# Half of the fifth-chunk adds as accumulating transfers, value sums in four batches, and the second tile's copies on swapped engines

## The chip, the core and the metric

The kernel runs on one core of a Trainium2 chip. The core has five engines that run in parallel, each through its own queue in order: TensorE (PE, with its weight load PEld), VectorE (DVE), ScalarE (ACT), GpSimd (POOL) and SyncE (SP), which only issues transfers. They meet at semaphores. The metric is the device time of one execution in microseconds (us); all times below are in us unless marked ns. The kernel before takes 266.07, the median of three runs (266.06 to 266.19).

## The reference

A layer norm feeds a sliding attention and a gated product; both are added to the input.

```python
xn = _layernorm(x)                       # x: [1, 2048, 640], bf16
qkv = xn @ wqkv                          # 32 heads of 20
idx = pos[:, None] - 2 * arange(8)       # each position sees 8 earlier ones, 2 apart
logits = einsum("bhsd,bhswd->bhsw", q, kg) * 20 ** -0.5     # masked where idx < 0
o = einsum("bhsw,bhswd->bhsd", softmax(logits), vg)
a = o.reshape(1, 2048, 640) @ wo
b = ((xn @ w_gate) * (xn @ w_up)) @ w_down                  # inner width 1536
return x + a + b
```

## The kernel before

**An order written by a planner.** The program is built by a small list scheduler (`Sched`, lines 50 to 351). Every operation is given to it with a planned cost (`occ`, `acc`), and what it reads and writes. Threads (Python generators) offer tasks with a priority; `run` (line 235) picks, engine by engine, the task that can start first by the planned costs, and among those within a small patience the one of best priority. What comes out is a fixed list of instructions for each engine, with a semaphore wait wherever a result of another engine is needed. The planned costs thus set the order alone; on the chip an instruction waits for its data and for nothing else. `slack` on a task moves its planned readiness later, `keep` asks that so many PSUM banks stay free besides its own. `lock=True` keeps DVE passes over 16-bit data in SBUF and POOL's adds from running at the same time.

**Tiles.** The 2048 positions are 16 tiles of 128 (`TS`) and four blocks of 512 (`JB`, index j); the 640 features are five chunks of 128 (`NCH`, index c). PSUM has eight banks of 512 fp32 columns.

**Start.** A tile t is loaded, DVE takes its statistics, ACT the square root, and DVE applies the norm (`front`, line 566). For tiles 0 to 3 TensorE transposes the five chunks and they are copied from PSUM to `XNT`. For tiles 0 and 1 this goes in two parts, chunks 0 and 1, then 2 to 4 (`PARTS`, line 502), and `COPY` (line 503) names the engine of each part. The first projections (`proj_group`, `spread`, line 730) follow a tile's parts. Ahead of all this `warm` (line 680) lets TensorE multiply zeros.

**Logits.** A query is multiplied with its eight shifted keys on DVE, in two halves r of four shifts. For blocks 0 and 1 a product of one chunk is one pass in bf16 (`narrow`, L880), and five chunks are added by TensorE (L1012), through a matrix that also sums over a head. For blocks 2 and 3 (`QUAD`, line 424) only chunk 4 is done so. Chunks 0 to 3 are multiplied straight from PSUM into fp32 (`wide`, L929), in quarters (r, q0) of two shifts each, and are added by POOL, until one tile for each r is left for TensorE:

- the sum of chunks 0 and 1 (`sum32`, p = 0): an add on POOL (L955), or an accumulating transfer SBUF to SBUF issued from POOL's queue (L951), as `BY_DMA` says;
- then the fifth chunk's product `z` (bf16) is added to it (L966); `LAST_DMA`, which is empty, names the quarters where a transfer does it (L962);
- the sum of chunks 2 and 3, or of the running sum with chunk 2 (`close`, with `sum32` at p = 1), again by POOL or by a transfer;
- the closing add (L988), which writes bf16.

The logits of blocks 2 and 3 are one task for TensorE (`JOIN`, line 1468; `logits`, line 995), with a slack of 2.0. Softmax runs over two blocks at a time (`softmax`, line 1042).

**Values.** A unit u is a block and a chunk, u = 5j + c. DVE multiplies the shifted values with the attention weights (L1191), POOL adds pairs of shifts (two adds per unit, L1196), and TensorE sums over the shifts left (L1250), whose result ACT evicts into `OT` (L1259). `BATCH` (line 1105) says after which units TensorE takes a batch of sums (`sums`, line 1237). A batch takes one PSUM bank per unit at once, and two more banks hold attention weights until the last unit is multiplied.

**Gate, up and down.** `gu` (line 1287) takes the gate and up projections of block j in twelve slices m (L1314), ACT evicts the gate, DVE multiplies (L1323, from PSUM). For slices in `FAST` (line 1467) ACT evicts the up part as well, and DVE multiplies in bf16 from SBUF (L1361). `dn` (line 1387) takes the down projection in pieces of a tile and 320 columns: twelve matmuls over `WD`, then five over `WO` with `OT` (L1416). A down piece keeps the banks of the next batch of sums free as long as the block's `OT` is not complete. Blocks 0 to 2 are added onto a copy of x in the output by an accumulating transfer from POOL's queue (`add_out`, line 1439); block 3 adds x on DVE (L1429) and is stored.

Of the kernel before, what the change touches and what calls it, by code (L numbers as in the profile page):

```python
# [15 lines left out]
NF = 12  # L16
# [5 lines left out]
TS = 128  # L22
JB = 512
HB = 1024
QB = 256
# [24 lines left out]
class Sched:  # L50
# [78 lines left out]
    def op(self, eng, fn, r=(), w=(), dma=False, name="", occ=None, lat=None, lock=False, nbytes=0, mode=0, group=None, extra=0.0, acc=0.0, land=None):  # L129
# [19 lines left out]
        if dma:  # L149
            self.t[eng] = start + (0.48 if occ is None else occ)  # L150
            if acc:
                self.t_acc = max(self.t_acc, start + 3.8) + acc
                X.end = self.t_acc
            else:
                self.t_data = max(self.t_data, start + 1.2) + nbytes / 280e3
                X.end = self.t_data + 0.8 + extra
# [199 lines left out]
def build_kernel(nc, A_x, A_wqkv, A_wo, B_x, B_w_gate, B_w_up, B_w_down, out):  # L356
# [68 lines left out]
    LAST_DMA = ()  # L425
# [77 lines left out]
    COPY = (("act", "act"), ("act", "dve"))  # L503
# [176 lines left out]
    def warm(n):  # L680
        for _ in range(n):
            op("pe", lambda e: e.matmul(PS[:, 7, 0:QB], ZERO[:, 0:128], ZERO[:, 0:QB], start=True, stop=True),
               r=[ZERO[:]], w=[PS[:, 7, :]], name="warm", occ=0.2 if n > 3 else 0.12)
# [80 lines left out]
    def proj_qk():  # L764
# [8 lines left out]
        for t in (4, 6):  # L773
            yield have("xnt", t + 1)
            for items in ([(0, 0, 2)], [(1, 0, 2)], [(0, 2, 2)], [(1, 2, 2)], [(0, 4, 1), (1, 4, 1)]):
                K.spawn(proj_group(items, t * TS, 2 * TS, 11 + t * 0.1, None))
# [68 lines left out]
    def products():  # L845
        rows = {j: [] for j in range(NJ)}
        joined = []
        holds = {}
        for at, (j, kind) in enumerate(ORDER):
# [4 lines left out]
            else:  # L854
                if len(QUAD.get(j, ())) == 2 and j not in holds and (j, "w") == ORDER[at + 1]:
                    yield from fetch(j, 0, holds.setdefault(j, {c: [] for c in range(4)}))
                for r in (1, 0):
                    for c in range(NCH - 1 if r in QUAD.get(j, ()) else 0, NCH):
                        yield from narrow(j, r, c, rows[j])
            if len(rows[j]) == 10 - 4 * len(QUAD.get(j, ())) and kind == ("w" if j in QUAD else "n"):  # L860
                if j in JOIN:
                    joined.append((j, rows[j]))
                    if len(joined) == len(JOIN):
                        K.spawn(logits(*joined))
                else:
                    K.spawn(logits((j, rows[j])))
# [43 lines left out]
    def wide(j, slots, hold):  # L910
        halves = [(r, q0) for r in QUAD[j] for q0 in (0, 2)]
        acc, parts = {}, {1: [], 0: []}
        lastc = {r: [n, 0] for n, _, r in slots}
        slots.clear()
# [32 lines left out]
    def sum32(j, r, q0, p, a, b, last=None):  # L947
        x, y = PRD32[a][:], PRD32[b][:]
        name = f"qsum{j}_{r}_{q0}_{p}"
        if (r, q0) in BY_DMA[p]:  # L950
            yield Task("pool", lambda: op("pool", lambda e: e.dma_start(x, y, accum_op=ALU.add), r=[x, y], w=[x], dma=True,  # L951
                                          name=name, occ=0.88, acc=3.4), r=[x, y], w=[x], prio=4)
# [8 lines left out]
        if (r, q0) in LAST_DMA:  # L961
            yield Task("pool", lambda: op("pool", lambda e: e.dma_start(x, z, accum_op=ALU.add), r=[x, z], w=[x], dma=True,  # L962
                                          name=name + "c", occ=0.88, acc=3.4), r=[x, z], w=[x], prio=4)
# [141 lines left out]
    BATCH = (4, 9, 14, 17, 19)  # L1105
# [131 lines left out]
    def sums(us):  # L1237
# [26 lines left out]
        yield Task("pe", go, r=[SV[sv_of[u]][:] for u in us], prio=9.7, banks=len(us), slack=0.7)  # L1264
# [135 lines left out]
    def dn_piece(j, t, nb, rows, c0, c1):  # L1400
# [38 lines left out]
        def add_out():  # L1439
# [3 lines left out]
                             name=f"oadd{j}", occ=0.88, acc=4))  # L1443
# [23 lines left out]
    FAST = [(1, m) for m in range(6, NF)] + [(2, m) for m in range(4, 8)]  # L1467
    JOIN = (2, 3)
# [26 lines left out]
    warm(18)  # L1495
# [64 lines left out]
```

## Time and profile before

| | |
|---|---|
| median of three runs | 266.07 |
| the profiled execution's own time | 266.25 |
| its span | 264.4 |
| PE busy | 259.8 (98% of the span), 1748 matmuls |
| DVE busy | 220.1 (83%) |
| POOL busy | 160.8 (61%) |
| ACT busy | 111.9 (42%) |
| value products L1191 on DVE | 54, 90.8 |
| value adds L1196 on POOL | 40, 94.4 |
| fifth-chunk adds L966 on POOL | 8, 19.5 |
| accumulating transfers L951 | 8 of 512 KB, median 5.1 to landing |

A busy share is an average over the whole span. The chain of work that ended last is followed back from the last instruction: at each step to what released it, or to the instruction before it on its engine. In the rows of the order in time the columns are start, busy time, engine, line, operation, output and inputs with their shapes (partitions x elements), a count of merged instructions, and in brackets the idle time of the engine just before and what ended it. A group's row gives the count, then busy time in total, the mean ns of one, and the idle time before them. Matmuls are pipelined, and the end of a matmul in the records is modelled; the pace is read from start to start.

### The profile page before, as it was taken

How to read it: one execution, taken by the hardware profiler on the slowest of the kernel's cores; microseconds unless marked ns; L12 is line 12 of the kernel's file. 1: busy time of each engine (PE TensorE's matmuls, PEld its weight loads, DVE VectorE, ACT ScalarE, POOL GpSimd, SP SyncE). 2: the span in 40 equal slices, each digit the busy share in tenths (PEclk: the TensorE clock that was granted, in tenths of full speed). 3: DMA queues.
4: the chain of work that ended last, by engine and by line, in shares of the span. 5: the costliest groups of instructions: out<-in, count | busy, mean ns of one | idle time of the engine just before them, and what ended most of it. 6: DMA issues, size and time to landing. Idle time of an engine off the chain costs nothing.

```text
span 264.4 us, 4405 instructions
## 1 busy us (share of the span) xinstructions
PE 259.8 (98%) x1748; PEld 151.8 (57%) x1748; DVE 220.1 (83%) x259; ACT 111.9 (42%) x203; POOL 160.8 (61%) x97
## 2 busy tenths in 40 slices
PE   7999999999999999999999999999999999999996
PEld 4896975444444444444444444477646775776675
DVE  4787899999998799778779999999899998995032
ACT  3468987556612221224268652531235134213100
POOL 3000000000599998899973575599999999999300
DMA  6964679960379995470249425736586537600711
GB/s 207 373 211 84 126 95 383 443 233 18 121 136 187 234 222 111 85 144 1 61 132 308 90 47 121 152 86 157 153 166 138 147 93 124 129 1 0 102 50 50
DMA packets 39685, 37.83 MB, mean 143 GB/s; under 512 B 15697, under 2 KB 37329, under 8 KB 39633
## 3 DMA queue, kind: packets, MB, share of 16 engines
q1 hardware_dynamic: 36688, 31.32, 44.3%
q0 software_dynamic: 2736, 6.16, 13.5%
q8 instruction: 13, 0.21, 0.4%
q10 hardware_dynamic: 240, 0.07, 0.1%
q14 instruction: 8, 0.06, 0.1%
HBM read 25.07 MB, written 7.23 MB: 122 GB/s over the span
## 4 chain that ended last, share of the span: by engine, by line
PE 96%; DMA 2%; DVE 1%; SPq 0%; ACT 0%; issue 0%
PE PS L1314 39%; PE PS L1416 28%; PE PS L698 23%; PE PS L1012 2%; PE PS L1250 2%; PE PS L730 2%; DMA XST<-in_A_x_dram 2%; DVE STATS L574 0%; PE PS L642 0%; SPq L480 0%; ACT XNT L655 0%; DVE XNS L603 0%; ACT SD L584 0%; DVE FB L1429 0%; DVE MV L577 0%
## 5 line engine op out<-in xcount | busy, mean ns | idle before, releaser
L1196 POOL TENSOR_TENSOR SV<-PV 128x1024 bf16<-128x1024 f32 x40 | 94.4, 2384 | 17.1 <-DVE PV L1191 5.9
L1191 DVE TENSOR_TENSOR PV<-VX,PS 128x1024 f32<-128x1024 bf16 (+1 forms) x54 | 90.8, 1730 | 1.5 <-POOL SV L1196 1.5
L698 PE MATMUL PS<-XNT,WQKV 128*128 128x512 bf16 (+2 forms) x390 | 60.8, 316 | 0.0
L1314 PE MATMUL PS<-XNT,WG 128*128 128x512 bf16 x240 | 59.7, 379 | 0.0
L1314 PE MATMUL PS<-XNT,WU 128*128 128x512 bf16 x240 | 59.6, 379 | 0.0
L698 PEld LDWEIGHTS PS<-XNT,WQKV 128*128 128x128 bf16 x390 | 37.9, 112 | 21.9 <-ACT LOG L1023 0.8
L1314 PEld LDWEIGHTS PS<-XNT,WG 128*128 128x128 bf16 x240 | 23.2, 98 | 28.9 <-DVE XNT L1323 0.8
L1314 PEld LDWEIGHTS PS<-XNT,WU 128*128 128x128 bf16 x240 | 23.5, 98 | 28.0
L929 DVE TENSOR_TENSOR PRF<-PS,KT 128x1024 f32<-128x1024 f32 x32 | 37.9, 1218 | 0.3 <-PE PS L698 0.3
L955 POOL TENSOR_TENSOR PRF<-PRF,PRF 128x1024 f32<-128x1024 f32 x8 | 22.0, 2755 | 20.6 <-DVE LOG L1072 20.6
L703 ACT ACTIVATE HT<-PS 128x512 bf16<-128x512 f32 x24 | 14.3, 597 | 34.5 <-PE PS L1314 34.5
L1416 PE MATMUL PS<-WD,HT 128*128 128x320 bf16 x192 | 28.7, 299 | 0.0
L703 ACT ACTIVATE FB<-PS 128x320 bf16<-128x320 f32 x24 | 10.5, 437 | 40.4 <-PE PS L1416 40.4
L880 DVE TENSOR_TENSOR PRD<-QT,KT 128x2048 bf16<-128x2048 bf16 x24 | 27.3, 1222 | 0.0
L1031 POOL MEMSET LOG<- 32x6 bf16 (+6 forms) x7 | 0.4, 95 | 44.2 <-ACT LOG L1023 44.2
L1416 PE MATMUL PS<-WO,OT 128*128 128x320 bf16 (+2 forms) x165 | 26.5, 295 | 0.0
L1416 PEld LDWEIGHTS PS<-WD,HT 128*128 128x128 bf16 x192 | 18.8, 98 | 7.6
L988 POOL TENSOR_TENSOR PRD<-PRF,PRF 128x1024 bf16<-128x1024 f32 x8 | 21.5, 2768 | 0.1
L966 POOL TENSOR_TENSOR PRF<-PRF,PRD 128x1024 f32<-128x1024 f32 x8 | 19.5, 2543 | 0.0
L1416 PEld LDWEIGHTS PS<-WO,OT 128*128 128x128 bf16 x165 | 16.0, 98 | 5.8
L1323 DVE TENSOR_TENSOR HT<-HT,PS 128x512 bf16<-128x512 bf16 x18 | 12.3, 686 | 7.0 <-PE PS L1314 7.0
L1429 DVE TENSOR_TENSOR FB<-PS,XR 128x320 bf16<-128x320 f32 (+2 forms) x9 | 4.1, 454 | 16.5 <-PE PS L1416 16.5
(72 smaller groups left out, 247.1 us busy)
## 6 DMA issues: line engine op xcount, KB each, us to landing
VX<-v_scratch SPq DMA_DIRECT2D x80, 130.0 KB, 3.1
PRF<-PRF POOLq DMA_DIRECT2D x8, 512.0 KB, 5.1
XST<-in_A_x_dram SPq DMA_DIRECT2D x16, 160.0 KB, 5.4
v_scratch<-VST SPq DMA_DIRECT2D x4, 640.0 KB, 6.5
WG<-in_B_w_gate_dram SPq DMA_DIRECT2D x1, 1920.0 KB, 8.8
WU<-in_B_w_up_dram SPq DMA_DIRECT2D x1, 1920.0 KB, 12.2
out_dram<-in_A_x_dram SPq DMA_DIRECT2D x1, 1920.0 KB, 19.7
WD<-in_B_w_down_dram SPq DMA_DIRECT2D x1, 1920.0 KB, 8.2
```

Source lines behind the costliest of these rows:

```text
L698: op("pe", (lambda o, l, x, c, first: lambda e: e.matmul(o, l, x, start=first, stop=(c == NCH - 1)))(o, l, x, c, first), r=[l, x], w=[o], ...
L703: X = op("act", (lambda o, i: lambda e: e.activation(o, i, ACT.Copy))(o, i), r=[i], w=[o], name=name, occ=0.12 + n * 0.9e-3)
L880: op("dve", lambda e: e.tensor_tensor(s[:], qb, kv, ALU.mult), r=[q, rk], w=[s[:]], name=f"prod{j}_{r}_{c}", occ=1.15, lock=True)
L929: X = op("dve", lambda e: e.tensor_tensor(o[:], qb, kv, ALU.mult), r=[q, rk, ("qev", j, c)], w=[o[:]], name=f"prow{j}_{r}_{c}_{q0}", occ=1.17)
L955: yield Task("pool", lambda: op("pool", lambda e: e.tensor_tensor(x, x, y, ALU.add), r=[x, y] + tokens(), w=[x], name=name, occ=2.36, lock ...
L966: yield Task("pool", lambda: op("pool", lambda e: e.tensor_tensor(x, x, z, ALU.add), r=[x, z] + tokens(), w=[x], name=name + "c", occ=2.36 ...
L988: yield Task("pool", lambda: op("pool", lambda e: e.tensor_tensor(o, a, y, ALU.add), r=[a, y] + tokens(), w=[o], name=f"qend{j}_{r}_{q0}", ...
L1191: last[0] = op("dve", lambda e: e.tensor_tensor(p, vw, a, ALU.mult), r=[vv] + rk, w=[p], name=f"pv{u}_{x}_{r0}", occ=0.09 + 1.1 * nr)
L1196: X = op("pool", lambda e: e.tensor_tensor(o, p[:, :, 0, :], p[:, :, 1, :], ALU.add), r=[p[:]] + tokens(), w=[o], name=f"pva{u}_{x}", occ= ...
L1314: op("pe", (lambda l, x, c: lambda e: e.matmul(PS[:, b, :], l, x, start=(c == 0), stop=(c == NCH - 1)))(l, x, c), r=[l, x], w=[PS[:, b, :] ...
L1323: X = op("dve", lambda e: e.tensor_tensor(h, h, PS[:, hold[1], :], ALU.mult), r=[h, PS[:, hold[1], :]], w=[h], name=f"h{m}_{j}", occ=0.65)
L1416: op("pe", (lambda l, x, i: lambda e: e.matmul(dst, l, x, start=(i == 0), stop=(i == n - 1)))(l, x, i), r=[l, x], w=[PS[:, b, :]], name=f" ...
```

## The change

- The planner's costs: an accumulating transfer is planned to land no sooner than 1.6 after its start plus its own time, instead of 3.8; its own time is 3.1 instead of 3.4 for the adds of products, 4.6 instead of 4 for the output.
- `LAST_DMA` names the quarters (1, 2) and (0, 2): in each of blocks 2 and 3, two of four fifth-chunk adds become accumulating transfers from bf16 into fp32.
- `COPY` for the second tile: DVE copies chunks 0 and 1, ACT chunks 2 to 4; it was the other way round.
- `warm`: 9 matmuls of 512 columns instead of 18 of 256.
- `BATCH` takes the five units of block 3 as one batch instead of three and two, and the slack of a batch is 4.0 instead of 0.7.
- `FAST` has the first four slices of block 3 as well.
- The other edits let `JOIN` hold several groups and `QUAD` hold one half of a block alone. With the values set here (`QUAD` both halves of blocks 2 and 3, `JOIN` one group) they select the same work as before.

```diff
             if acc:
-                self.t_acc = max(self.t_acc, start + 3.8) + acc
+                self.t_acc = max(self.t_acc, start + 1.6) + acc
...
     QUAD = {2: (1, 0), 3: (1, 0)}
-    LAST_DMA = ()
+    LAST_DMA = ((1, 2), (0, 2))
     BY_DMA = (((0, 0), (0, 2)), ((1, 0), (1, 2)))
...
-    COPY = (("act", "act"), ("act", "dve"))
+    COPY = (("act", "act"), ("dve", "act"))
...
-    def warm(n):
+    def warm(n, cols=QB):
         for _ in range(n):
-            op("pe", lambda e: e.matmul(PS[:, 7, 0:QB], ZERO[:, 0:128], ZERO[:, 0:QB], start=True, stop=True),
-               r=[ZERO[:]], w=[PS[:, 7, :]], name="warm", occ=0.2 if n > 3 else 0.12)
+            op("pe", lambda e: e.matmul(PS[:, 7, 0:cols], ZERO[:, 0:128], ZERO[:, 0:cols], start=True, stop=True),
+               r=[ZERO[:]], w=[PS[:, 7, :]], name="warm", occ=0.4 if cols > QB else 0.12)
...
             for items in ([(0, 0, 2)], [(1, 0, 2)], [(0, 2, 2)], [(1, 2, 2)], [(0, 4, 1), (1, 4, 1)]):
-                K.spawn(proj_group(items, t * TS, 2 * TS, 11 + t * 0.1, None))
+                if 1 not in QUAD or items[0][0] or items[0][1] == 4:
+                    K.spawn(proj_group(items, t * TS, 2 * TS, 11 + t * 0.1, None))
...
                 for r in (1, 0):
+                    if (r in QUAD.get(j, (r,) if kind == "n" else ())) != (kind == "n"):
+                        continue
...
-            if len(rows[j]) == 10 - 4 * len(QUAD.get(j, ())) and kind == ("w" if j in QUAD else "n"):
-                if j in JOIN:
-                    joined.append((j, rows[j]))
-                    if len(joined) == len(JOIN):
-                        K.spawn(logits(*joined))
-                else:
-                    K.spawn(logits((j, rows[j])))
+            if len(rows[j]) == 10 - 4 * len(QUAD.get(j, ())) and kind == ("n" if j not in QUAD else "w" if len(QUAD[j]) > 1 else "m"):
+                group = next((g for g in JOIN if j in g), (j,))
+                joined[group] = joined.get(group, ()) + ((j, rows[j]),)
+                if len(joined[group]) == len(group):
+                    K.spawn(logits(*joined[group]))
...
-        lastc = {r: [n, 0] for n, _, r in slots}
-        slots.clear()
+        lastc = {r: [n, 0] for n, _, r in slots if r in QUAD[j]}
+        slots[:] = [e for e in slots if e[2] not in QUAD[j]]
...
             yield Task("pool", lambda: op("pool", lambda e: e.dma_start(x, y, accum_op=ALU.add), r=[x, y], w=[x], dma=True,
-                                          name=name, occ=0.88, acc=3.4), r=[x, y], w=[x], prio=4)
+                                          name=name, occ=0.88, acc=3.1), r=[x, y], w=[x], prio=4)
...
             yield Task("pool", lambda: op("pool", lambda e: e.dma_start(x, z, accum_op=ALU.add), r=[x, z], w=[x], dma=True,
-                                          name=name + "c", occ=0.88, acc=3.4), r=[x, z], w=[x], prio=4)
+                                          name=name + "c", occ=0.88, acc=3.1), r=[x, z], w=[x], prio=4)
...
-    BATCH = (4, 9, 14, 17, 19)
+    BATCH = (4, 9, 14, 19)
...
-        yield Task("pe", go, r=[SV[sv_of[u]][:] for u in us], prio=9.7, banks=len(us), slack=0.7)
+        yield Task("pe", go, r=[SV[sv_of[u]][:] for u in us], prio=9.7, banks=len(us), slack=4.0)
...
-                             name=f"oadd{j}", occ=0.88, acc=4))
+                             name=f"oadd{j}", occ=0.88, acc=4.6))
...
-    FAST = [(1, m) for m in range(6, NF)] + [(2, m) for m in range(4, 8)]
-    JOIN = (2, 3)
+    FAST = [(1, m) for m in range(6, NF)] + [(2, m) for m in range(4, 8)] + [(3, m) for m in range(4)]
+    JOIN = ((2, 3),)
...
-    warm(18)
+    warm(9, JB)
```

More of the change, by code (lines that the diff above doesn't have):

```diff
@@ L846, in products @@
         rows = {j: [] for j in range(NJ)}
-        joined = []
+        joined = {}
         holds = {}
```

## The prediction

> **What bounds the kernel now.** I read the share of each engine first, then the chain that ended last, then the waits, and then the order of time around each edit.
>
> ```profile
> PE 259.8 (98%) x1748; PEld 151.8 (57%) x1748; DVE 220.1 (83%) x259; ACT 111.9 (42%) x203; POOL 160.8 (61%) x97
> PE 96%; DMA 2%; DVE 1%; SPq 0%; ACT 0%; issue 0%
> 8.30 0.39 ACT XNT L655
> ...
> 8.74 2.99 PE PS L730 x50
> ...
> 222.33 1.19 PE PS L1250 x20
> ...
> 242.10 0.76 PE PS L1250 x12
> 242.86 5.00 PE PS L1416 x36
> 247.86 0.55 PE PS L1250 x8
> 248.40 13.75 PE PS L1416 x117
> ```
>
> From 8.74 to 262.15 every step of the chain is on TensorE, with no step of waiting between; the view of the waits, asked for PE after 8.75, lists none. The matmuls also run at their own pace: 136 of 320 columns take 18.47 in the chain (0.136 each), and five of 512 columns 1.08 (0.216 each), everywhere alike. So the kernel is 8.74 before TensorE is fed, 253.4 of TensorE without a hole, and 2.2 of last eviction and store. A change can gain only what starts TensorE sooner, what removes TensorE time, or what shortens the end; it can lose wherever TensorE, which runs its queue in order, meets something not ready.
>
> Around the edits, the order of time (start, busy time, engine):
>
> ```profile
> 8.30 0.38 ACT L655 ACTIVATE XNT<-PS 128x256 bf16<-128x256 bf16 x1 [0.96 <-PE PS L642]
> 8.58 0.70 ACT L703 ACTIVATE QT<-PS 128x640 bf16<-128x640 f32 x1
> 8.65 0.36 DVE L653 COPY XNT<-PS 128x384 bf16<-128x384 bf16 x1 [0.44 <-PE PS L642]
> ...
> 127.42 5.18 POOL L988 TENSOR_TENSOR PRD<-PRF,PRF 128x1024 bf16<-128x1024 f32 x2
> 132.57 4.68 POOL L1196 TENSOR_TENSOR SV<-PV 128x1024 bf16<-128x1024 f32 x2
> 134.15 1.05 PE L1012 MATMUL PS<-PRD,G 128*32 128x512 bf16 x16
> ...
> 243.96 2.86 POOL L1196 TENSOR_TENSOR SV<-PV 128x1024 bf16<-128x1024 f32 x1
> 247.79 0.61 PE L1250 MATMUL PS<-SV,SEL 128*32 128x512 bf16 x8
> ```
>
> The joined logits of blocks 2 and 3 start 1.55 after POOL's last closing add (132.60), and the last value sums 0.97 after POOL's last value add (246.82): POOL is the second bound, close behind TensorE twice, but never ahead of it.
>
> **The basis.** The profiled execution took 266.25, its span 264.4, so 1.85 lies around the span. The median shown is 266.07, 0.18 less. I take differences within the span off the median.
>
> **Second tile's copy (engines swapped).** The copy of the first two chunks feeds TensorE at 8.74. ACT needs 0.38 for it. DVE has not copied 256 columns here, but 384 in 358 ns and 640 in 492 (both copies of that form): 0.52 ns per column, so 0.29. Bounds: 0.24 (two thirds of 358, no fixed part) and 0.36 (no shorter than 384 columns), a gain of 0.14 to 0.02. I take the line through both rows: **-0.09**, first matmul near 8.65. ACT now has the other three chunks: 0.49 (its only 384-column copy, the first tile's) from 8.65 to 9.14, and TensorE wants them after ten matmuls of 0.06, at 9.25; 0.07 is left, and if that cover goes, the overshoot is the price, at most the 0.09. Behind it on ACT waits the eviction of QT, from 8.58 to about 9.14, done 9.84; ACT's next is at 10.08 (a square root that waits for DVE), so nobody is late.
>
> **Warm-up.** 18 matmuls of 256 columns become 9 of 512: the same columns, 3.46 from 1.27 to 4.73, and TensorE's next work is at 5.42. Nothing, behind 0.69 of cover. If the cover went, the row gives no more than one longer matmul, 0.43.
>
> **Value sums, four batches for five.** 12 and 8 matmuls become 20. By start-to-start times, 12 take 0.77, 8 take 0.55, 20 take 1.19 (222.26 to 223.45), and each entry costs 0.09 to 0.10 ahead of it (a switch of tile shape). (0.77+0.09)+(0.55+0.10)-(1.19+0.09) = **-0.22** of TensorE itself. In the chain's own pieces (0.76+0.55-1.19) it is -0.12, the other bound. I take 0.22, since nothing else can run in the entries.
>
> Where the batch goes: it needs block 3's last add. Down pieces of block 3 can fill in, but each takes a bank and the program keeps five for the batch, so three start before it: 3 x 12 x 0.136 = 4.9, from 241.94 (end of block 2's down) to 246.83. The last add ended at 246.82 in this trace. So even with no gain on POOL the batch waits about 0.1. Afterwards ACT evicts five banks (five took 2.56, the first 0.45 after the batch began), 3.0 in all, of which the batch covers 1.2; a bank is free after 1.05, and one more down piece is 1.63, so 0.2 at worst is open. The 4.0 of slack in the order can only put the batch later among other work; it makes no instruction wait.
>
> **Fifth-chunk adds.** Four of eight adds (2.54 mean, 2.31 start to start) leave POOL; four transfers come onto POOL's queue. An issue has 1.03 busy, and 0.61 to 0.75 passes from it to the next add (100.89 to 101.50, 73.72 to 74.48). POOL: 4 x 2.31 - 4 x 0.70 = 6.4 less in a stage that took 63.5 (69.11 to 132.57) and idled 2.3 in it. Value adds then start up to 6.4 sooner, unless DVE holds them. Worth nothing on TensorE, which is fed either way.
>
> ```profile
> L966 POOL TENSOR_TENSOR PRF<-PRF,PRD 128x1024 f32<-128x1024 f32 x8 | 19.5, 2543 | 0.0
> PRF<-PRF POOLq DMA_DIRECT2D x8, 512.0 KB, 5.1
> DMA to landing us min/median/max: 4.5/5.1/7.5
> ```
>
> No transfer here adds 16-bit data into 32-bit. Its lower bound is the quickest alike one, 4.5, as its target is the same 512 KB; its upper twice the slowest, 15. I take 5.1, the same target. It replaces 2.5 on POOL, so each of these halves closes at least 2.6 later; one half of each block now has two transfers in a row (10.2). The cover is POOL's other work in the block, some ten adds, 23. Queued behind a POOL wait for a transfer are all later adds; behind them the joined logits, and TensorE.
>
> The Trainium skill ("DMA: Bandwidth & Descriptors", Anatomy of one DMA) fits a transfer from POOL as 2.0 plus bytes at 436 GB/s, an estimate of 3.2 here; the eight rows, 4.5 to 7.5, say otherwise and decide. By the page the new transfers would be harmless; by the rows they are hidden but not free.
>
> **Planner's costs and slack.** An accumulating transfer is now planned at 1.6+3.1 = 4.7 instead of 7.2; the rows are 4.5 to 7.5. So consumers are placed up to 2.5 sooner, and the order has lost that reserve. The logits keep 2.0 of slack. Zero expected, the first rival otherwise. SP's loads behind the logits (down weights, landed 143.24, wanted 172) only move forward.
>
> **Four fast products of block 3.** DVE 4 x (0.69 - 0.42) = 1.1 less; ACT 4 x 0.60 = 2.4 more, in 157 to 172, where ACT is busy 6.85 of 15. The fast form is kept apart from POOL adds: in the trace it made POOL idle 0.6 to 0.9 each round and DVE 0.3. DVE is busy 14.3 of those 15, so this is about even, zero on TensorE behind POOL's gain.
>
> **Sum.** -0.09 - 0.22 = -0.31: **265.76**, say 265.8, and 265.6 to 266.0 with the bounds above.
>
> **Rivals.**
> - *Transfers late at the joined logits (slower).* A transfer that takes 7.5 is 2.8 beyond plan; less 2.0 slack, 0.8 of TensorE. Two in a row: 3.6. Middle 1.8: 267.6, up to 269.4. For it: four transfers in the first burst already took 5.3 to 7.5, and now six share it. Against: they followed each other at 3.3, twelve make 40 of POOL's 57. It decides from 0.84 of wait (0.31 gain and 0.53, which is 0.2%).
> - *The batch of five starves TensorE.* If POOL's value adds end 1.5 later than now, or the five evictions have no down piece beside them (3.0 - 1.2 = 1.8): 267.3 to 267.6. Against: POOL has less to do.
> - *Order of DVE, ACT or POOL upset in block 3's products*, banks freed late: two or three rounds of 0.5, 266.9. Against: bank cover held everywhere in the trace.
> - *Nothing gained:* the first stretch meets the next arrival (third chunk, weights) and the merged batch its evictions: 266.07.
> - *Faster by over 0.2%:* needs 0.53, while both gains at their upper bounds give 0.14+0.23 = 0.37. Only with 0.16 at the start that I don't see: 265.5.
>
> **How the numbers follow.** 0.2%, 0.53, is about what a measurement of this kernel tells from no change. Forecast 0.47, nothing gained 0.08: same 0.55. Late transfers 0.19, starved batch 0.10, upset order 0.09: slower 0.38. Faster 0.07. The range starts at 265.5 and reaches to 268.0, over the middle of the first rival and the whole of the next two; outside are the first rival's upper half (0.10) and half of faster (0.04).
>
> **What will show it.** Right: TensorE's first L730 of the second stretch at about 8.65; no PE waits after it; one batch of 20 value sums at the end, between 242 and 247; POOL's first value add near 126 to 128. Wrong: a hole before L1012 near 130 with a transfer or POOL as releaser, a hole around the last L1250, or PE starting the stretch at 8.74 still.

## The result, and the profile after

The changed kernel takes 268.39, the median of six runs (267.92 to 270.23), against 266.13 for the kernel before in the same comparison: a ratio of 1.0094, with a 95% interval of 1.0069 to 1.0118. It is slower by about 0.9%, and the forecast of 265.8 and its range up to 268.0 were both missed.

The profiled execution took 268.64 with a span of 266.9 (before 266.25 and 264.4). From the first multiplication after the second tile's copy to the end of the last piece of TensorE, the chain now runs from 8.90 to 264.66, which is 255.76; before it was 8.74 to 262.15, 253.41. I call this the *stretch*; it leaves out the start, which differs from run to run, and so compares two profiled executions better than their totals do. It grew by 2.35. The start gave 0.16 and the time around the span 0.11 less: 2.35 + 0.16 - 0.11 = 2.40, and the totals differ by 2.39.

The page of the changed kernel, shares of the engines and of the chain that ended last:

```profile
PE 261.0 (98%) x1739; PEld 151.3 (57%) x1739; DVE 218.4 (82%) x259; ACT 113.5 (43%) x207; POOL 156.0 (58%) x97
PE 72%; POOL 12%; DVE 8%; issue 3%; DMA 3%; ACT 1%; DVEq 0%; POOLq 0%
```

Before, TensorE held 96% of the chain; now POOL, DVE and a transfer hold 23% between them. TensorE did not become much idler on average (98% busy either way). But one short wait is enough to send the chain back through everything that made that wait. The list of TensorE's waits in the changed kernel has two that the kernel before had not:

```profile
PE PS L1251 <- DVE XNT L1324: 2.0, 1, 2.0
...
PE PS L1013 <- POOL PRD L989: 0.2, 1, 0.2
```

(L1251 sums the values, L1013 sums the logits; from about L880 on the changed file's line numbers are one higher than before.) The chain, start and length of each step, shows where both come from:

```profile
103.97 7.40 DMA PRF<-PRF
...
130.79 0.61 PE PS L1013 x8
...
162.43 2.37 POOL SV L1197
...
164.82 2.35 DVE PV L1192 x2
167.18 0.40 DVE XNT L1362
...
167.59 0.60 ACT UF L703
...
168.22 0.44 DVE XNT L1362
...
168.73 2.38 POOL SV L1197
...
171.54 0.69 DVE XNT L1324
...
172.28 0.40 PE PS L1251 x4
```

Read from the bottom up. TensorE's fifth unit of value sums starts at 172.28, when DVE's product (L1324) has emptied the bank that it needs. That product stands behind a fast one (L1362), which waits for POOL's value add of 168.73 to 171.10; the add waited for another fast product, that one for ACT's eviction, and this for an earlier product behind an earlier pair of adds. Far above, the chain leads to a transfer of 7.40 among the logits' adds. The order in time at the end of it, for TensorE and DVE (start, busy time; in brackets the idle time just before and what ended it):

```profile
169.22 1.05 PE L1251 MATMUL PS<-SV,SEL 128*32 128x512 bf16 x16
...
171.20 0.43 DVE L1362 TENSOR_TENSOR XNT<-XNT,ZERO 128x512 bf16<-128x512 bf16 x1 [1.42 <-ACT OT L1260]
172.28 0.40 PE L1251 MATMUL PS<-SV,SEL 128*32 128x512 bf16 x4 [2.01 <-DVE XNT L1324]
```

The trace names ACT for DVE's wait of 1.42, but the add on POOL, which ended at 171.10, comes 0.1 before the fast product, and `lock` keeps the two apart; in the chain the add is the step before. (So `lock` is not only a matter of the order: the kernel makes a semaphore wait of it, and on the chip too a fast product waits for the add ahead of it, although it reads nothing that the add writes.) From the first of these sums (169.22) to the next gate slice (172.67 in the chain) it is 3.45, where an undisturbed batch takes 1.19 + 0.09: a hole of **2.17**. The second hole, at the logits, is **0.35**. Against them stands what the merged batch saves, 0.22: 2.17 + 0.35 - 0.22 = 2.30 of the 2.35.

Two of the six runs took 269.9 and 270.23 with a mean granted clock of 0.994, the others 267.92 to 268.64 with 1.0; the section on e3 shows what that is.

What the new transfers did can be read from POOL's own order (between the logits' products and the first value add):

```profile
108.97 2.12 POOL L967 TENSOR_TENSOR PRF<-PRF,PRD 128x1024 f32<-128x1024 f32 x1 [0.29 <-DMA PRF<-PRF]
111.65 0.87 POOL L963 DMA_DIRECT2D PRF<-PRD  x1 [0.56 <-DMA PRF<-PRF]
...
115.62 0.86 POOL L952 DMA_DIRECT2D PRF<-PRF  x1 [2.20 <-DVE PRF L930]
...
130.57 4.72 POOL L1197 TENSOR_TENSOR SV<-PV 128x1024 bf16<-128x1024 f32 x2
```

and from two groups of transfers, and DVE's row for the fp32 products:

```profile
PRF<-PRF POOLq DMA_DIRECT2D x8, 512.0 KB, 7.6
PRF<-PRD POOLq DMA_DIRECT2D x4, 512.0 KB, 5.9
...
L930 DVE TENSOR_TENSOR PRF<-PS,KT 128x1024 f32<-128x1024 f32 x32 | 37.9, 1215 | 5.0 <-DMA PRF<-PRF 4.9
```

The old transfers' median rose from 5.1 to 7.6, DVE waited 4.9 for them (it waits for a buffer to be summed away before it writes the next product), and POOL stood still for 0.29, 0.56 and 2.20 behind transfers and the late products. POOL was busy 25.95 of the 30 between 100 and 130, before 28.02. The first value add started at 130.57 instead of 132.57: four adds fewer, but only 2.0 sooner.

The longest of these waits is DVE's for block 3's first transfer, which was issued at 101.05 and landed 7.84 later, at 108.89. DVE's row for it, and the shares of the 16 DMA engines by queue between 101 and 105 (q0 holds POOL's transfers, q1 here SP's loads; the shares add up the times of packets, which overlap):

```profile
108.91 1.22 DVE L930 TENSOR_TENSOR PRF<-PS,KT 128x1024 f32<-128x1024 f32 x1 [3.95 <-DMA PRF<-PRF]
...
q1 hardware_dynamic: 620, 0.57, 75.9%
q0 software_dynamic: 73, 0.30, 38.1%
```

No other transfer of POOL's was on its way when this one started; the last of the first burst had landed at 94.22. What it met were SP's loads of the shifted values, whose last one landed at 105.71; in the kernel before it landed at 101.26. The section on e4 shows that this is the transfer that the order had not reckoned with.

### The profile page after: what moved, and what is told of

The parts are those of the page before. It is cut to its first block, busy times and chain, and to the rows that moved or that the text cites. A ratio compares the mean times of both kernels' runs of the same rounds, so it can differ in the third digit from the quotient of the medians.

```text
span 266.9 us, 4381 instructions
## 1 busy us (share of the span) xinstructions
PE 261.0 (98%) x1739; PEld 151.3 (57%) x1739; DVE 218.4 (82%) x259; ACT 113.5 (43%) x207; POOL 156.0 (58%) x97
## 4 chain that ended last, share of the span: by engine, by line
PE 72%; POOL 12%; DVE 8%; issue 3%; DMA 3%; ACT 1%; DVEq 0%; POOLq 0%
PE PS L1417 28%; PE PS L698 22%; PE PS L1315 15%; POOL SV L1197 5%; POOL PRD L989 3%; DMA PRF<-PRF 3%; PE PS L730 2%; DVE PV L1192 2%; PE PS L1013 2%; POOL PRF L956 2%; PE PS L682 2%; PE PS L1251 1%; POOL PRF L952 1%; DVE PRF L930 1%; DVE SM L1046 1%
## 5 line engine op out<-in xcount | busy, mean ns | idle before, releaser
L1315 PE MATMUL PS<-XNT,WG 128*128 128x512 bf16 x240 | 59.7, 379 | 0.0
L1315 PE MATMUL PS<-XNT,WU 128*128 128x512 bf16 x240 | 59.6, 379 | 0.0
L1315 PEld LDWEIGHTS PS<-XNT,WG 128*128 128x128 bf16 x240 | 23.3, 98 | 28.5 <-ACT LOG L1024 0.4
L1315 PEld LDWEIGHTS PS<-XNT,WU 128*128 128x128 bf16 x240 | 23.4, 98 | 28.1 <-issue 0.2
L956 POOL TENSOR_TENSOR PRF<-PRF,PRF 128x1024 f32<-128x1024 f32 x8 | 19.3, 2427 | 20.8 <-DVE LOG L1073 20.6
L989 POOL TENSOR_TENSOR PRD<-PRF,PRF 128x1024 bf16<-128x1024 f32 x8 | 19.0, 2400 | 0.3
L574 DVE BATCH_NORM_STATS2 STATS<-XST 128x6 f32<-128x320 bf16 x32 | 14.0, 470 | 2.3 <-DMA XST<-in_A_x_dram 2.3
L1324 DVE TENSOR_TENSOR HT<-HT,PS 128x512 bf16<-128x512 bf16 x18 | 12.3, 681 | 2.9 <-PE PS L1315 2.9
```

Of the source, the lines that this page charges most:

```text
L574: op("dve", lambda e: e.bn_stats(o, a), r=[a], w=[("st", t, i)], name=f"bn{t}_{i}", occ=0.49)
L956: yield Task("pool", lambda: op("pool", lambda e: e.tensor_tensor(x, x, y, ALU.add), r=[x, y] + tokens(), w=[x], name=name, occ=2.36, lock ...
L989: yield Task("pool", lambda: op("pool", lambda e: e.tensor_tensor(o, a, y, ALU.add), r=[a, y] + tokens(), w=[o], name=f"qend{j}_{r}_{q0}", ...
L1315: op("pe", (lambda l, x, c: lambda e: e.matmul(PS[:, b, :], l, x, start=(c == 0), stop=(c == NCH - 1)))(l, x, c), r=[l, x], w=[PS[:, b, :] ...
L1324: X = op("dve", lambda e: e.tensor_tensor(h, h, PS[:, hold[1], :], ALU.mult), r=[h, PS[:, hold[1], :]], w=[h], name=f"h{m}_{j}", occ=0.65)
```

## The experiments

Each is a small edit of the changed kernel (after) or of the kernel before. The table gives the median, its ratio to the kernel before on the same chip with the 95% interval, the stretch of the profiled execution against 253.41, and the holes in TensorE's work that make the difference, read from start to start. Where the last batch is merged, 0.22 comes off.

| kernel | median | ratio [95%] | stretch | holes, us |
|---|---|---|---|---|
| after | 268.39 | 1.0094 [1.0069, 1.0118] | +2.35 | 2.17 at 170, 0.35 at the logits |
| e1, after without the new transfers | 266.94 | 1.0030 [1.0018, 1.0043] | +1.10 | 1.32 at 225 |
| e2, after without block 3's fast products | 266.32 | 1.0001 [0.9985, 1.0018] | -0.05 | 0.17 at 169 |
| e3, after with the old warm-up | 267.92 | 1.0063 [1.0040, 1.0086] | +3.82 | 2.18 at 169, then half pace, 1.7 |
| e4, after with the old planned costs | 267.53 | 1.0043 [1.0028, 1.0057] | +1.52 | 0.37 at the logits, 1.32 at 225 |
| e5, before + the new transfers | 266.57 | 1.0018 [1.0007, 1.0030] | +0.42 | 0.41 at the logits |
| e6, before + the new warm-up | 266.09 | 0.9997 [0.9986, 1.0009] | +0.13 | 0.11 at 11 |
| e8, before + four batches + slack 4.0 | 267.56 | 1.0058 [1.0039, 1.0077] | +1.11 | 1.32 at 225 |
| e10, before + block 3's fast products | 266.36 | 1.0003 [0.9986, 1.0021] | 0.00 | none |
| e13, before + four batches + swapped copy | 265.69 | 0.9994 [0.9975, 1.0013] | -0.22 | none |
| e14, before + slack 4.0 | 266.18 | 1.0001 [0.9985, 1.0018] | 0.00 | none |
| e15, after, last fast products not kept from POOL's adds | 270.66 | 1.0160 [1.0123, 1.0198] | +4.55 | 3.06 at 169, then half pace |
| e16, after with old costs and five batches | 266.79 | 1.0020 [1.0003, 1.0038] | +0.95 | 0.37 at the logits, 0.55 at 253 |

Ahead of the first four runs I held three theories. Theory 1: the new transfers run late against the order, and POOL, DVE and TensorE fall behind it. Theory 2: the fast products of block 3, which may not run beside POOL's adds, make the hole at 170 whatever the transfers do. Theory 3: the new warm-up lets TensorE reach its full pace later. That the hole needs the transfers, the order and the fast products together is what came out of these runs. Each of the four puts one part back.

### e1: the new transfers taken out

```diff
-    LAST_DMA = ((1, 2), (0, 2))
+    LAST_DMA = ()
```

> The changed kernel with no fifth-chunk add by transfer (four adds back on POOL), all else kept. Theory 1 (the added transfers run late against the order, POOL and DVE fall some 4 us behind it, and TensorE meets a bank not yet freed, 2.17, and a logits operand, 0.35): both holes go, 268.4 - 2.5 = 265.9. Theory 2 (the four fast products of block 3, which may not run beside a POOL add, make the hole whatever the transfers do): the hole of about 2 before the fifth unit's sums stays, 268.0 to 268.4.

Measured: 266.94, and both holes of the changed kernel are gone, as theory 1 said, but the time is 1.0 above its 265.9. A new hole appears, between 223.5 and 226.5. The chain of e1 there:

```profile
221.93 1.63 PE PS L1417 x12
223.56 0.36 PE PS L1251 x4
...
223.94 2.56 ACT OT L1260 x5
...
226.55 21.36 PE PS L1417 x156
```

A down piece of block 2 has begun (twelve matmuls over `WD`) before block 2's batch of sums; its other five, over `WO`, each need one of the five evictions that ACT makes of that batch, 0.5 apart. TensorE's order holds nothing else between, so it waits 0.26 + 3 x 0.354 = 1.32, and 1.32 - 0.22 for the merged batch is the whole +1.10. So the transfers are needed for the hole at 170, and the change holds a second trap, which the order of the changed kernel as a whole happens to escape.

### e2: block 3's fast products taken out

```diff
-    FAST = [(1, m) for m in range(6, NF)] + [(2, m) for m in range(4, 8)] + [(3, m) for m in range(4)]
+    FAST = [(1, m) for m in range(6, NF)] + [(2, m) for m in range(4, 8)]
```

> The changed kernel with block 3's first four products on DVE from PSUM again, all else kept. Theory 1: POOL and DVE are as late as before (first value add near 130.6), and a hole of 1 to 2 near 170 stays, 267.4 to 268.4. Theory 2: the hole near 170 goes, the 0.35 before the logits stays, 266.2.

Measured: 266.32, ratio 1.0001, stretch -0.05; theory 2 had said 266.2. The order in time of e2 where the hole was:

```profile
167.38 7.00 POOL L1197 TENSOR_TENSOR SV<-PV 128x1024 bf16<-128x1024 f32 x3 [1.64 <-DVE PV L1192]
...
168.65 1.43 PE L1251 MATMUL PS<-SV,SEL 128*32 128x512 bf16 x20
...
168.95 0.68 DVE L1324 TENSOR_TENSOR XNT<-XNT,PS 128x512 bf16<-128x512 bf16 x1
```

POOL runs three adds in a row and DVE multiplies beside them from PSUM: the plain product (L1324) takes its 0.68 while an add runs. Twenty sums take 1.43 instead of 1.26, and that 0.17 is all that is left of the hole: 0.17 - 0.22 is the -0.05. So the fast products are needed for it too, and taking them out of the changed kernel wins back the whole loss. One thing is not theirs: the 0.35 at the logits is missing in e2 as well, where 16 matmuls take 0.98 without a wait, and up to there both kernels have the same order. Four profiled executions have this order up to the logits: the changed kernel loses 0.35 there, e3 0.17, e2 and e15 nothing. So the 0.35 varies from one execution to the next.

### e3: the old warm-up

```diff
-    warm(9, JB)
+    warm(18)
...
-               r=[ZERO[:]], w=[PS[:, 7, :]], name="warm", occ=0.4 if cols > QB else 0.12)
+               r=[ZERO[:]], w=[PS[:, 7, :]], name="warm", occ=0.2 if n > 3 else 0.12)
```

> The changed kernel with 18 warm-up matmuls of 256 columns again. Theory 3 (nine of 512 columns let TensorE reach its full pace later: near 7.2 in the changed kernel's trace, near 4.0 before): the first stretch after the second tile's copy starts at 8.65 instead of 8.90, the time falls by 0.25 and the runs near 270 vanish, 268.1. Rival (the moment of full pace differs from run to run whatever the warm-up): no change of the median, 268.4, and single slow runs stay.

Measured: 267.92; the interval of its ratio (1.0040 to 1.0086) overlaps that of the changed kernel, and the hole is there as before (2.18). The warm-up as the cause of the hole falls; that it costs nothing by itself is shown by e6. The profiled execution, 269.57, showed something else. Windows of e3 (their length, busy time and count of TensorE, its weight load, DVE, ACT and POOL, then the granted clock, the DMA share and GB/s):

```profile
171.70:175.30 3.60, 3.60 (x15) 1.59 (x12) 3.60 (x2) 0.60 (x1) 3.16 (x2) 0.53 0.13 29
175.30:185.00 9.70, 9.70 (x74) 6.97 (x72) 9.70 (x6) 1.75 (x4) 9.39 (x5) 1.00 0.43 112
```

After the hole TensorE's granted clock is 0.53 for 3.6, and its matmuls run at half pace; the order in time gives `171.77 2.31 PE L1315` for five that take 1.25 elsewhere. By the granted clock these 3.6 lose 3.6 x 0.47 = 1.7: 2.18 + 1.7 - 0.22 = 3.7 of the +3.82 (its logits, 1.15 long instead of 0.98, are 0.17 more). The mean clock of this run is 0.994, as in the two long runs of the changed kernel.

### e4: the old planned costs

```diff
-                self.t_acc = max(self.t_acc, start + 1.6) + acc
+                self.t_acc = max(self.t_acc, start + 3.8) + acc
...
-                                          name=name, occ=0.88, acc=3.1), r=[x, y], w=[x], prio=4)
+                                          name=name, occ=0.88, acc=3.4), r=[x, y], w=[x], prio=4)
...
-                             name=f"oadd{j}", occ=0.88, acc=4.6))
+                             name=f"oadd{j}", occ=0.88, acc=4))
```

(the 3.4 for both kinds of the adds)

> The changed kernel with the planner's old costs of accumulating transfers (3.8 + 3.4, and 4 for the output), all else kept, so the same twelve transfers in an order that allows for 7.2 us each. Theory 1, in the form that the order trusts the transfers too much: holes gone, 266.0. Theory 1, in the form that the transfers themselves collide with SP's loads, whatever the order: POOL still late, 267 to 268.4. Theory 2: 268.0 to 268.4.

Measured: 267.53, where the theory had 266.0. Same transfers, same fast products, but an order planned for slower transfers: no hole at 170. The joined logits now wait (rows of e4, order in time):

```profile
134.98 2.37 POOL L1197 TENSOR_TENSOR SV<-PV 128x1024 bf16<-128x1024 f32 x1
...
135.18 0.40 PE L1013 MATMUL PS<-PRD,G 128*32 128x512 bf16 x4 [0.21 <-ACT LOG L1024]
```

The trace names ACT for the wait of 0.21, but POOL's last closing add ended at 135.03, just before it, and in e16, at the same place, the trace names POOL. POOL's first value add is at 134.98, later than the 132.57 of the kernel with four transfers fewer. And the trap of e1 is back: 1.32 at 225. Together 0.37 + 1.32 - 0.22 = 1.47 of +1.52.

From e1, e2 and e4 the hole at 170 needs three parts at once: the transfers, the order planned for quick ones, and block 3's fast products. None of e1, e2 or e4 has it; e3, which has all three, does.

Late against what, if POOL's first value add of the changed kernel (130.57) comes sooner than that of every kernel in the table but e2, e3 and e15, which share its order up to there? Late against its own order. The starts that the planner reckons with can be worked out from each kernel's code (they are its estimates, not times of the chip). POOL's first value add, planned and measured, and the same for the add beside the hole, POOL's eleventh:

| kernel | first value add | eleventh | late | hole at 170 |
|---|---|---|---|---|
| after | 126.76, 130.57 | 164.12, 168.73 | 3.8, 4.6 | 2.17 |
| e3 | 126.76, 129.77 | 164.12, 167.90 | 3.0, 3.8 | 2.18 |
| e2 | 126.76, 129.21 | 164.86, 167.38 | 2.5, 2.5 | 0.17, no fast product there |
| e1 | 132.32, 130.88 | 168.57, 169.97 | -1.4, 1.4 | none |
| e4 | 134.22, 134.98 | 171.33, 173.44 | 0.8, 2.1 | none |
| e10 | 132.49, 132.73 | 168.74, 170.52 | 0.2, 1.8 | none |

TensorE started these sums 0.4 to 1.3 later than planned in all six. In the changed kernel the plan had 1.3 between the end of DVE's product (167.47) and the fifth unit of sums (168.74), and its add ran 3.3 later than its TensorE: that leaves a wait of 2.0, which is what the trace has (2.01).

The planner's code also tells where it was wrong. It lets the transfers of a burst land one after the other, 3.1 apart, so block 2's six were planned at 4.7, 6.9, 9.1, 9.0, 8.9 and 8.7, and took 5.0, 6.4, 8.9, 9.4, 8.3 and 8.4: right to within 0.9 at the landing. Block 3's first two were planned at 4.7 and took 7.84 and 7.40; the first landed 4.3 after its plan. The trace says why. In every kernel with the new transfers, e5 with nothing else among them, SP's loads ran on until 104.6 to 106.3 (before 101.26, e1 100.70). Under the new costs (the changed kernel, e2, e3, e15) block 3's first transfer was issued beside them, at 100.4 to 101.1, and took 6.7 to 7.8; under the old costs (e4, e5, e16) it came when they were done or nearly so, at 104.6 to 105.6, and took 4.5 to 4.6.

### e8, e14 and e13: where the trap at 225 comes from

e8 puts the batch edits alone into the kernel before, e14 the slack alone, e13 the merged batch without the slack (and the swapped copy).

```diff
-    BATCH = (4, 9, 14, 17, 19)
+    BATCH = (4, 9, 14, 19)
...
-        yield Task("pe", go, r=[SV[sv_of[u]][:] for u in us], prio=9.7, banks=len(us), slack=0.7)
+        yield Task("pe", go, r=[SV[sv_of[u]][:] for u in us], prio=9.7, banks=len(us), slack=4.0)
```

> The kernel before with four batches of value sums and the slack of 4.0, and nothing else. The prediction's term: 265.8 (-0.22), no hole. Rival (a down piece is put ahead of a batch, takes the last bank, and its second half then waits for the evictions, as in two runs where it cost 1.06): 266.9.

Measured: 267.56, with e1's hole to the hundredth. TensorE in e8 (one more row like the last two follows at 226.78):

```profile
223.72 1.26 PE L1250 MATMUL PS<-SV,SEL 128*32 128x512 bf16 x20
224.91 0.71 PE L1416 MATMUL PS<-WO,OT 128*128 128x320 bf16 x2
225.80 0.31 PE L1416 MATMUL PS<-WO,OT 128*128 128x320 bf16 x1 [0.18 <-ACT OT L1259]
226.29 0.31 PE L1416 MATMUL PS<-WO,OT 128*128 128x320 bf16 x1 [0.18 <-ACT OT L1259]
```

e14, the slack alone:

```diff
-        yield Task("pe", go, r=[SV[sv_of[u]][:] for u in us], prio=9.7, banks=len(us), slack=0.7)
+        yield Task("pe", go, r=[SV[sv_of[u]][:] for u in us], prio=9.7, banks=len(us), slack=4.0)
```

> The kernel before with a slack of 4.0 for the value sums and the old five batches. If the slack makes the hole at the evictions (a down piece goes ahead of a batch and holds the last bank): 1.06 of holes near 225, 267.1. If the larger last batch makes it: no hole, 266.0.

Measured: 266.18, stretch +0.00. TensorE in e14 at the same place:

```profile
223.96 1.26 PE L1250 MATMUL PS<-SV,SEL 128*32 128x512 bf16 x20
225.15 1.26 PE L1416 MATMUL PS<-WD,HX 128*128 128x320 bf16 x8
```

Here too the slack lets one down piece begin ahead of the batch. But a second piece (8 matmuls over `HX`) follows the sums and covers ACT's evictions. The difference between the two is how many banks a piece must leave free for the *next* batch (`keep=next_sums`): three in e14, five in e8. That a second piece finds room with three reserved and not with five is read from the code; that the order differs there, and costs 1.32, is shown.

e13 leaves the slack at 0.7:

```diff
-    COPY = (("act", "act"), ("act", "dve"))
+    COPY = (("act", "act"), ("dve", "act"))
...
-    BATCH = (4, 9, 14, 17, 19)
+    BATCH = (4, 9, 14, 19)
```

> The kernel before with four batches of value sums at the old slack of 0.7, and the second tile's copies swapped: the prediction's two gains and nothing else. If the terms hold: the first matmul after the second tile's copy 0.09 sooner after its transposes, one batch of 20 at the end instead of 12 and 8, no hole, 266.0 - 0.3 = 265.7. If five banks at the end cost more than the switch they save: a hole of 0.4 to 1.1 beside the last batch, 266.2 to 266.9.

Measured: 265.69, ratio 0.9994 [0.9975, 1.0013]. The chain of e13 at the end:

```profile
222.18 1.19 PE PS L1250 x20
223.38 23.47 PE PS L1416 x172
246.85 1.19 PE PS L1250 x20
```

The third batch stands ahead of block 2's down pieces, the last begins at 246.85 (the prediction's working said 246.83), nothing in the stretch waits (gaps of 0.2 in the trace stand where a matmul has no record; 17 of 1748 have none), and it is 0.22 shorter, the predicted figure. The copy gave its share too: from the start of the second tile's first transposes to the first multiplication it is 0.67 (7.93 to 8.60), in the changed kernel 0.66 (8.24 to 8.90), and 0.76 in the kernel before (7.98 to 8.74). This is the best version found, 0.43 below its own comparison's median of 266.12, but within the scatter of those runs, so it is not shown to be faster by the clock; the trace shows 0.3 less work.

### e5 and e10: the transfers alone, the fast products alone

```diff
-    LAST_DMA = ()
+    LAST_DMA = ((1, 2), (0, 2))
```

> The kernel before with the four fifth-chunk adds by transfers and nothing else, planned at the old 7.2 us. If the transfers do harm in themselves (they share the DMA engines with SP's loads and with each other): 0.3 to 0.4 before the joined logits, 266.4, and more if a later bank is late. If they do harm only where the order trusts them too much: no hole, 266.0, no gain either, since TensorE has no wait to lose.

Measured: 266.57, ratio 1.0018 [1.0007, 1.0030]; POOL's first value add at 135.37, the joined logits 0.41 longer. In the kernel before, the transfers by themselves make POOL later by 2.8 (2.4 counted from the start of the stretch) and gain nothing. Most of it is planned: at the old costs the order itself puts this add at 134.39 instead of 132.49.

```diff
-    FAST = [(1, m) for m in range(6, NF)] + [(2, m) for m in range(4, 8)]
+    FAST = [(1, m) for m in range(6, NF)] + [(2, m) for m in range(4, 8)] + [(3, m) for m in range(4)]
```

> The kernel before with the four fast products of block 3 and nothing else. If these products make the hole only together with a POOL that runs behind the order: POOL's value adds stay within 0.5 of the order, no hole, 266.0. If they make it by themselves: a hole of 1 to 2 before the fifth unit's sums near 170, 267 to 268.

Measured: 266.36, stretch 0.00. The four fast products cost nothing by themselves. In e10 POOL's two adds at 164.37 end before the last fast products (169.08 and 170.03), and its next one comes after them, at 170.52; the order of the changed kernel has an add between two of them.

### e6: the warm-up alone

```diff
-    warm(18)
+    warm(9, JB)
```

(with the columns and the planned cost of `warm` as in the change)

> The kernel before with nine warm-up matmuls of 512 columns and nothing else. Theory 3: TensorE is still at half pace when the first transposes come, full pace between 5.5 and 7.2 instead of 4.0 to 4.5, the first tile's 25 matmuls end 0.3 to 0.7 later, and 0.1 to 0.4 of it reaches the end: 266.2 to 266.4. Rival (the moment depends on the run alone): 266.0, full pace near 4.

Measured: 266.09, ratio 0.9997. What looked like an effect of the warm-up in the profile after (transposes at slow pace until 7.2) varies from run to run. The windows from 5.5 to 6.5 of e5, with 18 short matmuls, and of e6, with 9 long ones, show TensorE first (busy time and count of its instructions). e5:

```profile
5.50:6.50 1.00, 1.00 (x9) 0.77 (x8) 0.26 (x1) 0.80 (x2) 0.00 (x0) 1.00 1.02 282
```

and e6:

```profile
5.50:6.50 1.00, 0.99 (x14) 0.73 (x15) 0.97 (x4) 0.76 (x2) 0.00 (x0) 1.00 0.84 239
```

Nine or fourteen in the same time: the slow one is here the old form. But the kernel before, also the old form, has 14, and the changed kernel, the new form, has 8. The pace does not go with the form.

### e15: fast products beside POOL's adds

The order keeps fast products and POOL's adds apart. e15 lifts this for block 3's slices in the changed kernel.

```diff
-                                name=f"h{m}_{j}", occ=0.34, lock=True)
+                                name=f"h{m}_{j}", occ=0.34, lock=j < 3)
...
-                        yield Task("dve", fmul, r=[h, us], prio=H_PRIO, lock=True)
+                        yield Task("dve", fmul, r=[h, us], prio=H_PRIO, lock=j < 3)
```

> The changed kernel with block 3's four fast products let loose from POOL's adds in the order (they need not wait for one any more), all else kept. If the hole near 170 comes through this link (a late POOL add holds a fast product, and that holds the product behind it and its bank): the hole falls from 2.2 to below 0.5, 266.2 to 266.7. If the hole comes from DVE or ACT being late without it: 1.5 to 2.2 stay, 267.7 to 268.4.

Measured: 270.66, the slowest of all, and outside of both expectations. Rows of e15:

```profile
163.82 2.54 POOL L1197 TENSOR_TENSOR SV<-PV 128x1024 bf16<-128x1024 f32 x1
...
165.20 1.45 DVE L1362 TENSOR_TENSOR XNT<-XNT,ZERO 128x512 bf16<-128x512 bf16 x1
...
168.83 0.41 DVE L1362 TENSOR_TENSOR XNT<-XNT,UF 128x512 bf16<-128x512 bf16 x1
```

The same fast product takes 0.41 while POOL waits (its next add begins at 168.99) and 1.45 beside an add; others beside adds took 1.67 and 1.44. So the wait is not an artefact of the order: kept apart, the product waits for the add; let loose, it takes more than three times as long. Three of them (1.67, 1.45 and 1.44 instead of 0.42) cost DVE 3.3 more, which is more than the hole that was to close. It grew to 3.06, and half pace followed it (granted clock 0.57 from 172.70 to 176.50): 3.06 + 1.7 - 0.22 = 4.54 of +4.55.

### e16: old costs and old batches

```diff
-    BATCH = (4, 9, 14, 19)
+    BATCH = (4, 9, 14, 17, 19)
```

and the edit of e4.

> The changed kernel with the planner's old costs and the old five batches, so that transfers, fast products, slack, copies and warm-up are those of the change. If the hole near 170 needs an order that trusts the transfers, and the 1.06 beside the third batch needs the five banks kept for the last one: both are gone, only some 0.4 before the joined logits is left, 266.4. If either comes from the transfers or the fast products themselves: 1 to 2 stay, 267.2 to 268.4.

Measured: 266.79, stretch +0.95. The holes at 170 and 225 are both gone, and 0.37 at the logits is left, as in e4 and e5. I had not foreseen the other 0.55. The chain of e16:

```profile
252.57 0.36 PE PS L1251 x4
...
252.95 0.61 ACT OT L1260
...
253.60 8.92 PE PS L1417 x81
```

With five batches and a slack of 4.0, the last batch of two comes after six down pieces of block 3 (five in e14) and the next piece finds no bank until ACT has evicted one. Why it is so in e16 and not in e14, which has the same slack and batches, was not settled.

## Why the prediction was wrong

**Second tile's copy, -0.09: right.** DVE's copy took 0.29, as taken from the line through the two other copies, and the part is 0.09 to 0.10 quicker. ACT's copy of the other three chunks took the expected 0.49 and nobody waited.

**Warm-up, zero: right** (e6).

**Merged batch, -0.22: right in size** (e13, -0.22), and the term is in every sum above. The starved last batch, one of the rivals, did not come.

**"The 4.0 of slack ... can only put the batch later among other work; it makes no instruction wait": wrong.** In an order written in advance, later among other work means that something else comes sooner, and here this was half a down piece whose second half needs the batch's evictions. With the merged batch it costs 1.32 (e8); with the old batches nothing (e14). The prediction looked at the bank cover of block 3's batch alone, and not at block 2's, on which the slack and the larger reservation act together. In the changed kernel itself the order happens to escape this trap: its third batch stands at 225.06 ahead of all 172 down matmuls.

**Fifth-chunk adds, "POOL 6.4 less", "value adds start up to 6.4 sooner": the size was wrong.** The four adds are gone from POOL, but the first value add came 2.0 sooner in the changed kernel, and 2.4 to 2.8 later than in the kernel before under the old costs (e4, e5). The term took 5.1 for a transfer, from a trace in which four shared the first burst. With six in it they took 5.0 to 9.4; the first two of block 3's took 7.8 and 7.4 (before 4.5 and 4.9). The prediction knew that the first burst had stretched transfers to 7.5, and kept the median. It looked at POOL's transfers among themselves and not at SP's loads, which the longer burst pushed from 101.26 to 105.71, into block 3's transfers. DVE waited 4.9 for a buffer behind transfers (3.95 of it in block 3), and POOL for DVE, which the term did not have. (Its lower bound of 4.5 was too high as well: one transfer from bf16 took 3.9.)

**Planner's costs, "zero expected": wrong.** The figure of 4.7 for 7.2 holds only for a transfer that finds the queue empty; queued ones are planned later, and block 2's landed as planned. Block 3's first two, planned at 4.7, took 7.8 and 7.4, and the first value add was 3.8 behind the order. The prediction said that the order had lost a reserve, and looked for the price only at the joined logits. There it was 0.35, well below the 1.8 of the first rival, and not in every execution. The lateness went on through POOL's value adds, and the chain reaches from the transfer at 103.97 to the hole at 172.

**Four fast products, "about even, zero on TensorE behind POOL's gain": wrong in company.** Alone they are zero (e10). The condition in that sentence, POOL's gain, stood in the order and came on the chip only in part: the order counted on a first value add 5.7 sooner (126.76 instead of 132.49), it came 2.0 sooner, and one of the late adds stands between two fast products, with a product and a bank behind them. The rival of banks freed late in block 3's products is what happened, with one hole of 2.17 instead of two or three rounds of 0.5. The prediction had argued against it that the bank cover held everywhere in the trace; but that trace had no fast product at that place.

The sum: -0.09 and -0.22 came; 2.17 and 0.35 were priced as rivals, each on its own and with a separate chance, while one cause, late transfers in an order that did not expect them, brought both. Some of the written sums are off in small ways that change nothing here: 9.25 less 9.14 leaves 0.11 and not 0.07, the batch's terms as written give 0.23, and the upper bounds of both gains end at 265.7 and not 265.6. What stays open: whether the batch edits matter for the hole at 170 was not tried (the slack does move these sums in the order: in e14, with the slack alone, they began at 174.15 instead of 169.76), and no run moved SP's loads alone.

## What to carry to other kernels

In an order fixed in advance, a planned cost is a promise: a transfer that is planned at 4.7 and takes 7.8 need not stall TensorE where it lands, but wherever the engine behind it meets a lock or a bank, 60 us later here. Compare planned starts with those of the trace, engine by engine: an engine can be earlier than in the kernel before and still be late. When transfers are added, look at what the other queues have under way at that time. Price edits that lower a reserve together with those that need it, not one by one; and before a task is moved by slack, list what takes its place on its engine and whether that needs the moved task's result. When parts of a change are mixed, put them back one at a time, and note what appears as well as what goes: here the second loss showed only once the first one's cause was taken out.

## What the hardware showed that I had not expected

- A DVE product of 128x512 in bf16 from SBUF takes 0.41 to 0.42 alone and 1.44 to 1.67 beside a POOL add, which itself goes from 2.35 to about 2.5 (e15), while the product with one operand in PSUM keeps its 0.68 beside an add (e2). The Trainium skill ("GPSIMD Engine Reference", Specifications) says that POOL shares its SBUF interfaces with VectorE and names contention with DVE instructions that read two SBUF inputs; the runs agree and give it a price.
- After a hole of 2 to 3 in TensorE's work, the next 3.6 to 3.8 ran at about half pace in the profiled executions of e3 (hole 2.18, granted clock 0.53) and e15 (3.06, 0.57), and not in that of the changed kernel (2.17, 1.00): about 1.7 more, in some executions only. The Trainium skill ("TensorE: Matmul & The Clock Gate", Part 1) lets the clock fall after about 3.4 of idleness; here a shorter hole was enough, and the measurement decides.
- The moment at which TensorE reaches full pace at the start differs between runs whose warm-up is the same: by the starts of its matmuls at 4.0 in the profiled execution of the kernel before and at 7.3 in that of e5, while the granted clock of these windows reads 1.00 in both. What it costs is not shown.
- Six accumulating transfers of 512 KB in one burst took up to 9.4 each, four up to 7.5, and block 3's in the kernel before, two at a time, 4.5 to 5.0. One without another of its queue beside it at its start, but with SP's loads holding 75.9% of the DMA engines' time, took 7.84.
